# An attention and feed-forward kernel on one core: the accumulator bank of the second layer's h gets a tile of its own, and the seven output sums are paired anew in the other tiles

## The chip, the cores and the metric

The kernel runs on one core of a Trainium2 chip. The metric is the device time of one execution in microseconds. The engines that matter are PE (TensorE, with its weight loads PEld), ACT (ScalarE), DVE (VectorE) and SP, which issues all DMAs. PE writes its sums into PSUM, which has eight banks of 128 partitions x 512 floats; ACT and DVE read and write them there.

## The reference, cut to what matters

```
x = chunked softmax attention(q, k, v)          # 4608 tokens x 512
h = x @ moe_w_in;   g = elu(h);        x = g @ moe_w_out      # first layer, 512 -> 2048 -> 512
h = x @ moe2_w_in                                             # second layer
g = where(h >= 1, h, where(h <= -1, 0, (h + 1)**2 / 4))
out = g @ moe2_w_out
```

## The kernel before, in words

Tokens go in nine blocks of 512. The first layer runs plainly: 12 matmuls of 128x512 per slice of h (L682) and 12 per slice into four sums (L712), each factor split into a high and a low part.

The second layer uses a 2x2 scheme with seven products in place of eight. For each block b it takes eight steps (s counts them, 72 in all). A step works on two 128-wide slices of the hidden layer and two halves of the tokens. Its **products** (L774, in `step2`) are summed in one PSUM bank, called `hb`, whose two halves of 256 columns serve as two running sums. PE issues four runs of products per step:

- `first`, 12 matmuls. ACT then copies half 1 aside to z (`aside`, L797) and copies half 0 over half 1 (`seed(1)`, L800).
- `second`, 12 matmuls. ACT then reads half 0 into raw (`keep`, L806) and copies half 1 over half 0 (`seed(0)`, L800).
- `third`, 12 matmuls. DVE then adds z to both halves into raw (`right`, L809).
- `fourth`, 6 matmuls. ACT then reads half 1 into raw (`keep`, L806); after that `first` of the next step may write.

ACT and DVE apply the activation to raw and split it into a high and a low part (L819 to L838). The **output matmuls** (L935, in `outs`) take these as operands: 42 per step, six for each of the seven sums `T["out"][0..6]`, each sum in a PSUM bank of its own. They stand between the runs of products of the step that follows, in pieces of 13 (sums 0, 1 and the first matmul of sum 2, behind `second`), 9 (behind `third`), 7 (behind `fourth`) and 13 (behind `first`). A step so has 84 matmuls of 128x256 on PE. The seven sums grow over the eight steps of a block; at its end ACT copies sums 0 and 2 (L977) and DVE adds sums 3, 4, 1 (L985) and, last, 5 and 6 (L1022) for the stores (L991), while the next block's products run on. ACT and DVE also prepare the next block's input then (L639, L643, L629).

A planner (`Plan`) places all operations by costs and due times, and so sets the order on each engine; its operations on the engine "X" only hand out buffers. The order is then written out, and a recording layer gives each instruction the semaphore waits that its tiles call for. A tile is what `ps` or `pair` returns: `ps("h", i, ...)` is one bank, `pair("a", i, ...)` and `pair("acc", i, ...)` two banks under one name. There are eight banks: tile a0 (2), h0 and h1 (1 each), acc0 and acc1 (2 each). The first layer and the attention use them first, and `shared_banks` hands them on to the second layer.

Of the kernel before, what the change touches and what calls it, by code (L numbers as in the profile page):

```python
# [16 lines left out]
P = 128  # L17
BLK = 512
# [89 lines left out]
def chunk_attention_moe_moe2(ctx, tc, qk, v, w1, w2, w3, w4, out):  # L108
# [18 lines left out]
    NU = NT // P  # L127
# [22 lines left out]
    T = {}  # L150
# [9 lines left out]
    def ps(tag, i, shape, name):  # L160
        T[name] = pp.tile(shape, F32, tag=f"{tag}{i}", name=f"{tag}{i}")
        return T[name]

    def pair(tag, i, name):

        return ps(tag, i, [P, 2, BLK], name)
# [940 lines left out]
    def shared_banks():  # L1107
        last = L1 - 1
        T["out"] = [None] * 7

        def front(i):
            two = pair("a", i, "two")
            T["hb"], T["out"][0] = two[:, 0], two[:, 1]

        def middle(*i):
            for k in range(2):
                T["out"][1 + k] = ps("h", i[k], [P, BLK], "one")

        def back(k):
            def fn(i):  # L1120
                two = pair("acc", i, "two")
                T["out"][k], T["out"][k + 1] = two[:, 0], two[:, 1]
            return fn

        yield Op("X", 0.0, front, after=[("x", NU - 1)], take=("a",), event="hb")
        yield Op("X", 0.0, lambda: None, after=[], event=("free", 0, 0))
        yield Op("X", 0.0, middle, after=[("in", last)], take=("h",) * 2, event=("free", 0, 1))
        yield Op("X", 0.0, lambda: None, after=[], event=("free", 0, 2))
        yield Op("X", 0.0, back(3), after=[("half", last)], take=("acc",), event=("free", 0, 3))
        yield Op("X", 0.0, lambda: None, after=[], event=("free", 0, 4))  # L1130
        yield Op("X", 0.0, back(5), after=[("out", last)], take=("acc",), event=("free", 0, 5))
        yield Op("X", 0.0, lambda: None, after=[], event=("free", 0, 6))

# [24 lines left out]
    with tc.manual_schedule():  # L1160
# [4 lines left out]
        p = Plan(BUFS)  # L1165
        p.add(0, shared_buffers())
        p.add(L1, shared_banks())
        p.add(-40, first_loads())
        for u in range(NU):
# [80 lines left out]
```

## Time and profile before

| | |
|---|---|
| median of 3 runs | 1690.82 us |
| the profiled execution, its own time | 1690.58 us |
| its span, from the first to the last instruction | 1688.8 us |
| second layer alone on PE | about 896 to 1682 us of the span |
| PE busy / PE weight loads busy | 96% / 85% of the span |
| DVE / ACT busy | 61% / 58% |
| DMA, mean over the span | 160 GB/s |

The time of an execution lies 1.8 us above its span. A row of the timeline joins neighbouring instructions of one line; its first number is the start, and in brackets stands how long its engine had been idle and what ended that. The ends of matmuls are modelled: a matmul's modelled end lies past the start of the next one, so that differences of starts are the surer measure on PE.

### The profile page before, as it was taken

The numbers are of one execution on the slowest core, as the hardware profiler recorded it, in microseconds if no ns is written. First come the engines' busy times: TensorE is split into PE (matmuls) and PEld (weight loads), VectorE is DVE, ScalarE is ACT, GpSimd is POOL, SyncE is SP. The second block draws the span as 40 slices with busy tenths as digits, with TensorE's granted clock in tenths as the row PEclk, the third lists the DMA queues.
The fourth block names the chain that finished last, engine by engine and source line by source line (L and its number), as shares of the span: only waits on it lengthen the run. The fifth ranks groups of instructions, "written<-read, shape, count | busy, mean of one in ns | idle before, by whom it ended". The sixth has DMA issues, their size and how long they took to land.

```text
span 1688.8 us, 30552 instructions
## 1 busy us (share of the span) xinstructions
PE 1620.3 (96%) x11952; PEld 1430.1 (85%) x11952; DVE 1034.1 (61%) x1902; ACT 983.1 (58%) x2008; POOL 0.7 (0%) x6
## 2 busy tenths in 40 slices
PE   6999999999999999999999999999999999999998
PEld 5788888888888888888888999898989898989897
DVE  8992555555565555656335675757575757575665
ACT  6883444544555554555335666666666766666664
POOL 0000000000000000000000000000000000000000
PEclk9999999999999999999999999999999999999999
DMA  8640332433343434424656565656565656566565
GB/s 288 202 135 1 119 100 88 150 113 121 129 126 125 129 116 130 138 83 137 213 187 193 176 210 170 212 174 213 171 215 169 208 179 201 184 189 189 169 193 162
DMA packets 172497, 270.45 MB, mean 160 GB/s; under 512 B 15168, under 2 KB 78656, under 8 KB 172352
## 3 DMA queue, kind: packets, MB, share of 16 engines
q1 hardware_dynamic: 172352, 268.50, 50.3%
q8 instruction: 94, 1.54, 0.4%
q14 instruction: 51, 0.42, 0.1%
HBM read 219.15 MB, written 49.28 MB: 159 GB/s over the span
## 4 chain that ended last, share of the span: by engine, by line
PE 89%; ACT 6%; DVE 4%; issue 1%; DMA 0%; SPq 0%; DVEq 0%; ACTq 0%
PE acc L712 24%; PE h L682 24%; PE a L774 19%; PE acc L935 10%; PE h L935 5%; PE a L935 4%; ACT raw L806 2%; PE a L522 1%; ACT v L819 1%; ACT xu L639 1%; PE a L460 1%; DVE m L985 1%; PE h L502 1%; ACT m L977 0%; ACT high L835 0%
## 5 line engine op out<-in xcount | busy, mean ns | idle before, releaser
L774 PE MATMUL a<-xu,w 128*128 128x256 f32 x3024 | 409.4, 283 | 10.6 <-ACT raw L806 6.9
L774 PEld LDWEIGHTS a<-xu,w 128*128 128x128 f32 x3024 | 378.3, 188 | 17.2 <-ACT raw L806 8.5
L712 PE MATMUL acc<-gh,w 128*128 128x512 f32 x1152 | 297.4, 396 | 0.3 <-ACT gh L700 0.3
L682 PE MATMUL h<-xh,w 128*128 128x512 f32 x1152 | 292.3, 395 | 2.9 <-ACT w L249 1.6
L682 PEld LDWEIGHTS h<-xh,w 128*128 128x128 f32 x1152 | 216.3, 188 | 54.6 <-ACT w L249 1.8
L712 PEld LDWEIGHTS acc<-gh,w 128*128 128x128 f32 x1152 | 215.9, 188 | 51.5 <-ACT gh L700 0.8
L689 ACT ACTIVATE t<-h 128x512 f32<-128x512 f32 x144 | 86.0, 597 | 277.6 <-DVE gl L703 177.5
L935 PE MATMUL acc<-w,high 128*128 128x256 f32 x1728 | 240.1, 281 | 0.8 <-DVE m L985 0.8
L826 DVE SCALAR_TENSOR_TENSOR raw<-v,raw 128x256 f32<-128x256 f32 (+1 forms) x216 | 110.5, 512 | 202.4 <-ACT v L823 200.9
L935 PEld LDWEIGHTS acc<-w,high 128*128 128x128 f32 x1728 | 220.5, 188 | 1.0 <-DVE m L985 1.0
L703 DVE TENSOR_TENSOR gl<-t,gh 128x512 fp32r<-128x512 f32 x144 | 99.3, 689 | 174.7 <-PE acc L712 159.6
L838 DVE TENSOR_TENSOR high<-raw,high 128x512 fp32r<-128x512 f32 (+1 forms) x288 | 169.9, 620 | 24.3 <-ACT high L835 18.6
L697 DVE SCALAR_TENSOR_TENSOR t<-t,h 128x512 f32<-128x512 f32 x144 | 98.9, 687 | 136.8 <-ACT t L693 136.1
L835 ACT ACTIVATE high<-raw 128x512 fp32r<-128x512 f32 (+1 forms) x288 | 153.4, 571 | 35.0 <-DVE raw L826 23.9
L712 PE MATMUL acc<-gl,w 128*128 128x512 f32 x576 | 165.1, 400 | 0.0
L682 PE MATMUL h<-xl,w 128*128 128x512 f32 x576 | 157.3, 394 | 0.0
L819 ACT ACTIVATE v<-raw,half 128x256 f32<-128x256 f32 (+1 forms) x216 | 122.9, 573 | 46.3 <-DVE raw L809 46.3
L682 PEld LDWEIGHTS h<-xl,w 128*128 128x128 f32 x576 | 108.4, 188 | 25.7
L700 ACT ACTIVATE gh<-t 128x512 fp32r<-128x512 f32 x144 | 90.0, 625 | 64.6 <-PE acc L712 57.3
L712 PEld LDWEIGHTS acc<-gl,w 128*128 128x128 f32 x576 | 106.1, 188 | 24.5
L935 PE MATMUL h<-w,high 128*128 128x256 f32 x864 | 125.8, 281 | 0.1
L935 PEld LDWEIGHTS h<-w,high 128*128 128x128 f32 x864 | 112.7, 188 | 0.3 <-DVE high L838 0.3
(91 smaller groups left out, 1507.5 us busy)
## 6 DMA issues: line engine op xcount, KB each, us to landing
w<-w4s SPq DMA_DIRECT2D x504, 256.0 KB, 2.8
raw<-w SPq DMA_DIRECT2D x32, 512.0 KB, 7.3
qk<-qk SPq DMA_DIRECT2D x32, 512.0 KB, 4.8
m<-w SPq DMA_DIRECT2D x64, 256.0 KB, 3.4
w<-w3s SPq DMA_DIRECT2D x28, 512.0 KB, 4.0
w3s<-m SPq DMA_DIRECT2D x48, 256.0 KB, 2.5
w4s<-m SPq DMA_DIRECT2D x48, 256.0 KB, 2.7
v<-v SPq DMA_DIRECT2D x36, 256.0 KB, 3.2
```

Source lines behind the costliest of these rows:

```text
L682: nc.tensor.matmul(h, lhsT=w[:, wi, c, :], rhs=x[:, c, :], start=n == 0, stop=n == 3 * NC_ - 1)
L689: nc.scalar.activation(sb("t", i, [P, BLK], F32, ("act", s)), T["h", s], AF.Relu, scale=-1.0)
L697: nc.vector.scalar_tensor_tensor(out=t, in0=t, scalar=-1.0, in1=T["h", s], op0=ALU.add, op1=ALU.max)
L700: nc.scalar.activation(sb("gh", i, [P, BLK], F32R, ("gh", s)), T["act", s], AF.Copy)
L703: nc.vector.tensor_sub(sb("gl", gi, [P, BLK], F32R, ("gl", s)), T["act", s], T["gh", s])
L712: nc.tensor.matmul(T["acc", 0, b, m], lhsT=w[:, wi, m, :], rhs=T[g, s], start=first and (wi, g) == (0, "gh"), stop=last and g == "gl",)
L774: nc.tensor.matmul(half(q), lhsT=w[:, wi, c, :], rhs=x[:, c, :], start=start and k == 0, stop=clean and k == 5, skip_group_check=True,)
L819: nc.scalar.activation(t, part(), AF.Relu, bias=half_bias, scale=0.5)
L826: nc.vector.scalar_tensor_tensor(out=part(), in0=T["tt", s, ev], scalar=1.0, in1=part(), op0=ALU.min, op1=ALU.max)
L835: nc.scalar.activation(to(), of(), AF.Copy)
L838: nc.vector.tensor_sub(to(), of(), top())
L935: nc.tensor.matmul(T["out"][k][:, j * HB:(j + 1) * HB], lhsT=operand(k, s, lo)[:, j * P:(j + 1) * P], rhs=T["wo", 7 * s + k][:, wi], start ...
```

## The change

Only `shared_banks` is changed, which decides in which tile each of the second layer's eight banks lies.

| bank | tile before | tile after |
|---|---|---|
| `hb` | a0, with sum 0 | an h tile, alone |
| sum 0 | a0, with `hb` | a0, with sum 4 |
| sum 1 | an h tile, alone | acc, with sum 2 |
| sum 2 | an h tile, alone | acc, with sum 1 |
| sum 3 | acc, with sum 4 | acc, with sum 5 |
| sum 4 | acc, with sum 3 | a0, with sum 0 |
| sum 5 | acc, with sum 6 | acc, with sum 3 |
| sum 6 | acc, with sum 5 | an h tile, alone |

```diff
-        def front(i):
-            two = pair("a", i, "two")
-            T["hb"], T["out"][0] = two[:, 0], two[:, 1]
-
-        def middle(*i):
-            for k in range(2):
-                T["out"][1 + k] = ps("h", i[k], [P, BLK], "one")
-
-        def back(k):
+        def one(i):
+            return ps("h", i, [P, BLK], "one")
+
+        def h_bank(i):
+            T["hb"] = one(i)
+
+        def single(i):
+            T["out"][6] = one(i)
+
+        def two(tag, x, y):
             def fn(i):
-                two = pair("acc", i, "two")
-                T["out"][k], T["out"][k + 1] = two[:, 0], two[:, 1]
+                t = pair(tag, i, "two")
+                T["out"][x], T["out"][y] = t[:, 0], t[:, 1]
             return fn
 
-        yield Op("X", 0.0, front, after=[("x", NU - 1)], take=("a",), event="hb")
-        yield Op("X", 0.0, lambda: None, after=[], event=("free", 0, 0))
-        yield Op("X", 0.0, middle, after=[("in", last)], take=("h",) * 2, event=("free", 0, 1))
-        yield Op("X", 0.0, lambda: None, after=[], event=("free", 0, 2))
-        yield Op("X", 0.0, back(3), after=[("half", last)], take=("acc",), event=("free", 0, 3))
...
+        def free(*ks):
+            return [("free", 0, k) for k in ks]
+
+        yield Op("X", 0.0, h_bank, after=[("in", last)], take=("h",), event="hb")
+        yield Op("X", 0.0, two("a", 0, 4), after=[("x", NU - 1)], take=("a",), events=free(0, 4))
+        yield Op("X", 0.0, single, after=[], take=("h",), events=free(6))
+        yield Op("X", 0.0, two("acc", 1, 2), after=[("half", last)], take=("acc",), events=free(1, 2))
+        yield Op("X", 0.0, two("acc", 3, 5), after=[("out", last)], take=("acc",), events=free(3, 5))
```

No instruction is added or removed. Inside the second layer no instruction changes its place on PE, ACT, DVE or SP; only the waits differ. At the change of layers, where `hb` now comes from an h tile that the first layer gives up late, the first step's runs of products move one place back among the first layer's last matmuls.

On PE, inside a block, where `second` ends and the piece of 13 output matmuls begins. In the names, xu and w0, w1 are operands, high0 and high1 the split activations, and the waits in brackets name the engine or the DMA queue whose semaphore is waited for. Before:

```order
L774 MATMUL a0_7492<-xu1_7523,w0_8_7926 128x256 [waits Activation_49]
L774 MATMUL a0_7492<-xu1_7523,w0_8_7926 128x256 x5
L774 MATMUL a0_7492<-xu1_7523,w1_7_8072 128x256 x6
L935 MATMUL a0_7492<-w1_3_7930,high0_3_7481 128x256 [waits DMAHW3_49,Activation_49]
L935 MATMUL a0_7492<-w1_3_7930,high0_3_7481 128x256 x3
L935 MATMUL a0_7492<-w1_3_7930,high0_3_7481 128x256 [waits DVE_49]
L935 MATMUL h1_8289<-w1_3_7930,high0_0_7478 128x256 [waits DMAHW4_49]
```

And after, at the same place:

```order
L774 MATMUL h1_8210<-xu1_7522,w0_8_7925 128x256 [waits Activation_49]
L774 MATMUL h1_8210<-xu1_7522,w0_8_7925 128x256 x5
L774 MATMUL h1_8210<-xu1_7522,w1_7_8071 128x256 x6
L935 MATMUL a0_8211<-w1_3_7929,high0_3_7481 128x256 [waits DMAHW3_49]
L935 MATMUL a0_8211<-w1_3_7929,high0_3_7481 128x256 x3
L935 MATMUL a0_8211<-w1_3_7929,high0_3_7481 128x256 [waits DVE_49]
L935 MATMUL acc1_8400<-w1_3_7929,high0_0_7478 128x256 [waits DMAHW4_49,Activation_49]
```

The wait of sum 0's first matmul for ACT is gone; before, it was for the `keep` (L806) that reads `hb` behind `second`. The wait for ACT that sum 1 now shows is for the activation's high part (L835), which sum 0's wait had covered.

On ACT, at the same place. v0 is a scratch tile of the activation. Before:

```order
L835 ACTIVATE high1_2_8374<-raw2_7477 128x512 [waits DVE_49]
L806 ACTIVATE raw0_7475<-a0_7492 128x256 [waits PE_49]
L800 ACTIVATE a0_7492<-a0_7492 128x256 [waits PE_49,Activation_49]
L819 ACTIVATE v0_8555<-raw0_7475,half_70 128x256
L835 ACTIVATE high0_3_7481<-raw0_7475 128x256 [waits DVE_49]
```

And after:

```order
L835 ACTIVATE high1_2_8374<-raw2_7477 128x512 [waits DVE_49]
L806 ACTIVATE raw0_7475<-h1_8210 128x256 [waits PE_49]
L800 ACTIVATE h1_8210<-h1_8210 128x256 [waits Activation_49]
L819 ACTIVATE v0_8555<-raw0_7475,half_70 128x256
L835 ACTIVATE high0_3_7481<-raw0_7475 128x256 [waits DVE_49,PE_49]
```

`seed(0)` (L800) no longer waits for PE, that is, for sum 0's six matmuls; the wait for PE that the last row gains is for the matmuls that read the old high0_3, and stood in L800's before.

On PE, in the first step of a block, around `fourth`, where sum 3 is begun and DVE still reads the old sum 5 (L1022). Before:

```order
L935 MATMUL acc1_8400<-w1_1_7847,high0_1_7479 128x256 [waits DMAHW3_49]
L935 MATMUL acc1_8400<-w1_1_7847,high0_1_7479 128x256 x3
L774 MATMUL a0_7492<-xu2_8202,w1_4_7961 128x256 [waits DVE_49]
L774 MATMUL a0_7492<-xu2_8202,w1_4_7961 128x256 x5
L935 MATMUL acc1_8400<-w1_1_7847,high0_5_7483 128x256 x2
```

And after:

```order
L935 MATMUL acc0_8403<-w1_1_7846,high0_1_7479 128x256 [waits DMAHW3_49]
L935 MATMUL acc0_8403<-w1_1_7846,high0_1_7479 128x256 x3
L774 MATMUL h1_8210<-xu2_8201,w1_4_7960 128x256 [waits DVE_49]
L774 MATMUL h1_8210<-xu2_8201,w1_4_7960 128x256 x5
L935 MATMUL acc0_8403<-w1_1_7846,high0_5_7483 128x256 [waits DVE_49]
```

Sum 3's last two matmuls gain a wait for DVE, for the L1022 that reads sum 5 in the same tile; that L1022 in turn gains a wait for PE, for sum 3's first four matmuls.

## Rows read from the trace of the kernel before

**Rows 1.** The page: busy time of each engine, and the chain that ended last.
```profile
PE 1620.3 (96%) x11952; PEld 1430.1 (85%) x11952; DVE 1034.1 (61%) x1902; ACT 983.1 (58%) x2008; POOL 0.7 (0%) x6
...
PE 89%; ACT 6%; DVE 4%; issue 1%; DMA 0%; SPq 0%; DVEq 0%; ACTq 0%
```

**Rows 2.** Stretches: start:end, length, busy PE, PEld, DVE, ACT, POOL, clock, DMA, GB/s.
```profile
400.00:800.00 400.00, 400.00 (x2689) 324.04 (x2688) 233.60 (x435) 205.00 (x392) 0.00 (x0) 1.00 0.38 123
1000.00:1200.00 200.00, 188.66 (x1535) 183.53 (x1534) 127.38 (x236) 131.29 (x292) 0.00 (x0) 1.00 0.61 190
```

**Rows 3.** Waits of PE, whole span: total us, times, longest us.
```profile
PE a L935 <- ACT raw L806: 35.1, 71, 0.7
...
PE a L774 <- ACT raw L806: 6.9, 8, 0.9
...
PE a L774 <- DVE raw L809: 2.8, 8, 0.4
...
PE acc L935 <- DVE m L985: 0.8, 1, 0.8
```

**Rows 4.** Timeline of one step inside a block, 1007 to 1020 us.
```profile
1006.98 1.66 ACT L835 ACTIVATE high<-raw 128x512 fp32r<-128x512 f32 x3
...
1007.62 1.58 PE L774 MATMUL a<-xu,w 128*128 128x256 f32 x12
...
1009.24 0.38 ACT L806 ACTIVATE raw<-a 128x256 f32<-128x256 f32 x1 [0.60 <-PE a L774]
1009.68 0.78 PEld L935 LDWEIGHTS a<-w,high 128*128 128x128 f32 x6 [0.68 <-ACT raw L806]
1009.68 0.99 PE L935 MATMUL a<-w,high 128*128 128x256 f32 x6 [0.47 <-ACT raw L806]
...
1010.50 0.99 PE L935 MATMUL h<-w,high 128*128 128x256 f32 x7
1010.76 0.37 ACT L800 ACTIVATE a<-a 128x256 f32<-128x256 f32 x1 [1.14 <-PE a L935]
...
1011.33 1.59 PE L774 MATMUL a<-xu,w 128*128 128x256 f32 x12
...
1012.96 0.69 DVE L809 TENSOR_TENSOR raw<-a,z 128x512 f32<-128x512 f32 x1 [0.51 <-PE a L774]
...
1013.82 0.87 PE L774 MATMUL a<-xu,w 128*128 128x256 f32 x6
...
1015.37 1.59 PE L774 MATMUL a<-xu,w 128*128 128x256 f32 x12
...
1018.34 1.58 PE L774 MATMUL a<-xu,w 128*128 128x256 f32 x12
...
1020.40 0.99 PE L935 MATMUL a<-w,high 128*128 128x256 f32 x6 [0.47 <-ACT raw L806]
```

**Rows 5.** Timeline around the change from one block to the next, 1228 to 1257 us.
```profile
1228.72 0.99 PE L935 MATMUL a<-w,high 128*128 128x256 f32 x6 [0.47 <-ACT raw L806]
...
1235.68 1.68 PE L774 MATMUL a<-xu,w 128*128 128x256 f32 x12 [0.87 <-ACT raw L806]
...
1240.80 0.98 PE L935 MATMUL a<-w,high 128*128 128x256 f32 x6 [0.47 <-ACT raw L806]
...
1244.71 0.69 DVE L809 TENSOR_TENSOR raw<-a,z 128x512 f32<-128x512 f32 x1 [1.21 <-ACT m L977]
...
1245.46 0.97 PE L774 MATMUL a<-xu,w 128*128 128x256 f32 x6 [0.35 <-DVE raw L809]
...
1252.49 0.97 PE L935 MATMUL a<-w,high 128*128 128x256 f32 x6 [0.67 <-ACT raw L806]
...
1256.37 0.68 DVE L1022 TENSOR_TENSOR m<-acc,m 128x512 f32<-128x512 f32 x1
```

More of the change, by code (lines that the diff above doesn't have):

```diff
@@ L1109, in shared_banks @@
         T["out"] = [None] * 7
-        def front(i):
-            two = pair("a", i, "two")
-            T["hb"], T["out"][0] = two[:, 0], two[:, 1]
-        def middle(*i):
-            for k in range(2):
-                T["out"][1 + k] = ps("h", i[k], [P, BLK], "one")
-        def back(k):
+        def one(i):
[5 more added lines that the diff above has]
+        def two(tag, x, y):
             def fn(i):
-                two = pair("acc", i, "two")
-                T["out"][k], T["out"][k + 1] = two[:, 0], two[:, 1]
-            return fn
-        yield Op("X", 0.0, front, after=[("x", NU - 1)], take=("a",), event="hb")
-        yield Op("X", 0.0, lambda: None, after=[], event=("free", 0, 0))
-        yield Op("X", 0.0, middle, after=[("in", last)], take=("h",) * 2, event=("free", 0, 1))
-        yield Op("X", 0.0, lambda: None, after=[], event=("free", 0, 2))
-        yield Op("X", 0.0, back(3), after=[("half", last)], take=("acc",), event=("free", 0, 3))
-        yield Op("X", 0.0, lambda: None, after=[], event=("free", 0, 4))
-        yield Op("X", 0.0, back(5), after=[("out", last)], take=("acc",), event=("free", 0, 5))
-        yield Op("X", 0.0, lambda: None, after=[], event=("free", 0, 6))
+                t = pair(tag, i, "two")
+                T["out"][x], T["out"][y] = t[:, 0], t[:, 1]
+            return fn
+        def free(*ks):
[5 more added lines that the diff above has]
+        yield Op("X", 0.0, two("acc", 3, 5), after=[("out", last)], take=("acc",), events=free(3, 5))
     def block(b, f0=0, f1=NF):
```

## The prediction

> **What bounds the kernel now.** I read the page first. PE is busy for 96% of the span and makes 89% of the chain that ended last; DVE and ACT are busy for about 60% [rows 1]. So only time on PE counts, and the question is whether PE has idle time that this change reaches. The stretches answer where to look: in the first layer PE is busy for 400 of 400 us, in the second for 188.66 of 200 [rows 2]. The first layer offers nothing; the second, some 785 us long, has gaps. The waits name them: 71 times, nearly once for each of the 72 steps, an output matmul into tile a waited for ACT's L806, 35.1 us in all; the other waits of PE there are 6.9, 2.8 and 0.8 us [rows 3].
>
> The timeline of one step shows that wait [rows 4]. `second` starts at 1007.62. ACT's `keep` (L806) starts at 1009.24, when the last product is in the bank, and takes 0.38. Only then, at 1009.68, does sum 0's first matmul start, and its weight load with it. Yet `keep` reads `hb`, and sum 0 is another bank: they share a tile, no data. The same tie binds ACT: `seed(0)` (L800) begins only at 1010.76, after sum 0's six matmuls.
>
> What does it cost per step? From 1011.33 to 1018.34 PE issues 12, 9, 6, 7, 12 and 13 matmuls, 59 in 7.01 us without a wait: 0.1188 us each. A step has 84, so 9.98 us; but sum 0 comes at 1009.68 and again at 1020.40, 10.72 us later. 0.74 us per step are lost. They lie here: `second` should hand over after 12 x 0.1188 = 1.43 us and does so after 2.06, a loss of 0.63; the six matmuls of sum 0 then take 0.82 in place of 0.71, since the first weight load is no longer hidden, a loss of 0.11. (The view of waits shows 0.47 for the 0.63, as matmul ends are modelled late.)
>
> At that restart a rule of the Trainium skill can be weighed. The row shows the weight load and its matmul starting together at 1009.68, the load's unit having been idle for 0.68 [rows 4]: nothing was loaded ahead during the wait. The skill (page "TensorE: Matmul & The Clock Gate", section "Step-by-step: what each phase is for") has PE pull weight loads ahead of matmuls still in flight. If that held across a semaphore wait, the 0.11 would have another cause and might stay, which is 71 x 0.11 = 7.8 us less gain; the trace speaks against it here.
>
> **The change part by part.** First, `hb` leaves tile a. Sum 0 no longer waits for `keep`, `seed(0)` no longer waits for sum 0. In 71 steps 0.74 us go: **52.5 us**.
>
> Where does the stall go, what is late next? `third` needs `seed(0)`. Counted from the start of `second`: `keep` starts at 1.62 and ends at 2.00, L800 follows (0.37) and is done by about 2.4; 0.06 later, the lag between L806's end and sum 0, PE can know it: 2.46. PE itself arrives at `third` after 25 matmuls, at 2.97. So 0.5 us of cover remain. Before `keep`, ACT has three L835 that end at 1008.64, 0.60 ahead of it [rows 4]. `fourth` needs `right`: L809 starts 1.63 after `third` (1011.33 to 1012.96), takes 0.69, and with 0.06 the bank is free at 2.38; PE arrives after 21 matmuls, at 2.49. That order of 2.38 and 2.49 is the same as before, since from `third` to the next `second` nothing changes. The next step's `second` follows `first` after 25 matmuls, also as before (1015.37 to 1018.34).
>
> Second, the block changes. From sum 0 at 1228.72 to 1240.80 and 1252.49 two steps take 23.77 us, 2.33 more than 2 x 10.72 [rows 5]. Part of this is `first` at 1235.68, idle for 0.87 behind a `keep` that stands on ACT behind the preparation of the next block's input. With the 0.16 that the view leaves out (0.63 - 0.47) and the restart's 0.11 it is 1.14, and the change doesn't touch it. The other 1.2 us come from ties that go or loosen: L809 idles until L977 has copied sum 0 from the same tile, which holds `fourth` for 0.35 more; L800 and all that follows it on ACT come earlier; sum 0's wait at 1252.49 is 0.67 in place of 0.47. I take 1.19 for each of the 8 changes of block: **9.5 us**, bounds 0 and 2.33 x 8 = 18.6.
>
> Third, the new pairs. Sum 3 now lies with sum 5. In the first step of a block PE begins sum 3 (four matmuls) ahead of `fourth`, and DVE must then read the old sum 5 (L1022) before sum 3's last two. L1022 can start when those four are in the bank. By `keep`'s 1.62 against 1.43 that is 0.19 after they are issued, that is, after `fourth` has started; it takes 0.68 [rows 5], and with 0.06 PE may go on 0.93 after `fourth` started, in place of 6 x 0.1188 = 0.71. That is 0.22 and a restart of 0.11, or 0.33 at 8 places: **-2.6 us**, bounds 0 and -2.6, as DVE's next work waits on ACT anyway. The other pairs read their partner early: sum 4 waits for the copy of sum 0, sum 5 for the adding of sum 3, each with a run of products in between; I count nothing, and if that cover were gone it would cost one such 0.33 each.
>
> Fourth, the end. In the last step no products lie between the outputs; sum 4 there waits 0.8 us for DVE to read its old partner, sum 3 [rows 3]. Now sum 5 waits for that reader, one sum later, so that six matmuls (0.71) cover most of it. But DVE's adding, not PE, closes the kernel. Between 0 and 1, I take **0.5 us**.
>
> Fifth, the change of layers. The first runs of products move back one place among first-layer matmuls that never let PE idle [rows 2]. **0**, bounds 1 us either way.
>
> Sum: 52.5 + 9.5 - 2.6 + 0.5 = 59.9 us. The profiled execution took 1690.58 (span 1688.8 and 1.8 around it), 0.24 below the median, so no correction: **1630.7 us**. Best end: 52.5 + 18.6 + 1 = 72, 1618.5. Worst end: no gain at the block changes, -2.6 and -1: 48.9, 1641.7.
>
> **The rivals.** *The wait moves to `third`, in part.* If ACT reaches `keep` later than now, `seed(0)` ends later; past 0.50 us PE stands at `third`. ACT is 66% busy in this layer [rows 2], and with a step 0.74 shorter 70%; for it speaks that L835 ends only 0.60 ahead of `keep`, against it that L835's inputs hang on the `third` before, whose distance to `keep` doesn't change. If half of the 0.74 went that way: 1690.6 - 26 - 7 = about 1657. Chance 0.07.
>
> *The change frees nothing*, because the order between the engines is kept by bank and the wait has another reason. Against it: the wait for ACT stands on sum 0's first matmul before and not after, and `hb` and sum 0 were never in one bank. Time 1690.6. The Trainium skill (page "PSUM — Partial Sum Buffer", section "PSUM bank collisions raise a hardware error") asks that engines be kept apart by bank and quadrant; by that alone the kernel before would already let sum 0 run beside `keep`, and there would be nothing to win. The 71 waits of [rows 3] say that here it is the tile that counts. Chance 0.03.
>
> *Slower: `seed(0)` becomes the bound of the step.* With PE, ACT and DVE running closer together, `third` would stand behind L800 on ACT in every step. It decides from the point where L800 ends 0.50 + 0.74 = 1.24 us later after `second` than in the sum above; there the time is the old one. At 1.7 us it costs 0.46 x 71 = 33 us, 1724. Nothing in [rows 4] comes near: all that stands ahead of L800 is done 0.60 early. Chance 0.03.
>
> **How the numbers follow.** Forecast 0.87, the rivals 0.07, 0.03 and 0.03. A measurement of this kernel can tell about 2% from no change, here 1657. The forecast lies below with all its range, the first rival half: faster 0.91; within 2% 0.06; slower 0.03. The range is the forecast's own, 1618 to 1642; it leaves out the 0.13 of the rivals.
>
> **What would show it.** Right: sum 0 follows `second` with no idle time, L800 follows L806 at once, and a step inside a block takes 9.98 us; the waits of PE keep one of about 0.9 us per block at `first`, and a new one of about 0.1 to 0.3 for L1022 appears. Wrong: a wait for L800 at `third`, steps above 10.1 us, 0.35 at `fourth` still there at block changes, or a second new wait for L985 or L977 by the new pairs. A granted clock below 1.00 would upset all; at 400 of 400 us busy it was 1.00 [rows 2].

## The result and the profile after

| | before | after |
|---|---|---|
| median of its runs | 1690.82 us (3 runs) | 1631.14 us (3 runs) |
| ratio after to before, 95% interval | | 0.9646 (0.9624 to 0.9668) |
| the profiled execution / its span | 1690.58 / 1688.8 us | 1631.14 / 1629.2 us |

Slow executions are left out: one before (5036.68 us), one after (1946.26 us, at a mean granted clock of 0.754) and the profiled one of late_all below (5759.90 us, at 0.262), whose trace is therefore of a second run. The kernel became 59.7 us faster, to 1631.14 us; 1630.7 us was forecast.

The page after, its busy times and its chain, against [rows 1]:

```profile
PE 1600.5 (98%) x11952; PEld 1426.9 (88%) x11952; DVE 1032.0 (63%) x1902; ACT 984.9 (60%) x2008; POOL 0.7 (0%) x6
...
PE 94%; DVE 2%; ACT 2%; DMA 1%; issue 0%; SPq 0%; DVEq 0%
```

ACT falls from 6% to 2% of the chain with the same busy time: not its work shrank but what waited for it. The stretch inside the second layer, after (start:end, length, busy PE, PEld, DVE, ACT, POOL, clock, DMA, GB/s), against [rows 2]:

```profile
1000.00:1200.00 200.00, 198.31 (x1662) 197.46 (x1661) 135.69 (x252) 141.85 (x315) 0.00 (x0) 1.00 0.66 205
```

PE is busy for 198.31 of 200 us, where it was 188.66, and gets 1662 matmuls done in place of 1535. The waits of PE after, against [rows 3]:

```profile
PE acc L460 <- DMA qk<-qk: 7.0, 3, 4.1
PE h L774 <- ACT raw L806: 6.8, 8, 0.8
```

The 35.1 us of output matmuls behind L806, the 2.8 behind L809 and the 0.8 behind L985 are gone from the view; what stays in the second layer is one wait of `first` per block and, as before, a single one of 0.9 us in its second step. One step in the timeline after, against [rows 4]:

```profile
1000.40 1.58 PE L774 MATMUL h<-xu,w 128*128 128x256 f32 x12
...
1001.71 0.78 PEld L935 LDWEIGHTS a<-w,high 128*128 128x128 f32 x6
1001.83 0.87 PE L935 MATMUL a<-w,high 128*128 128x256 f32 x6
1002.03 0.38 ACT L806 ACTIVATE raw<-h 128x256 f32<-128x256 f32 x1 [0.60 <-PE h L774]
...
1002.44 0.37 ACT L800 ACTIVATE h<-h 128x256 f32<-128x256 f32 x1
...
1003.37 1.59 PE L774 MATMUL h<-xu,w 128*128 128x256 f32 x12
...
1005.00 0.69 DVE L809 TENSOR_TENSOR raw<-h,z 128x512 f32<-128x512 f32 x1 [0.87 <-PE h L774]
...
1005.86 0.87 PE L774 MATMUL h<-xu,w 128*128 128x256 f32 x6
...
1006.77 0.39 ACT L806 ACTIVATE raw<-h 128x256 f32<-128x256 f32 x1 [0.32 <-PE h L774]
...
1010.38 0.87 PE L774 MATMUL h<-xu,w 128*128 128x256 f32 x6
```

Sum 0 starts 1.43 us after `second`, ahead of `keep`, with its weights loaded 0.12 earlier; L800 follows L806 by 0.41; from `second` to `second` (1010.38; the view ends there and counts 6 of its 12 matmuls) it is 9.98 us, the forecast. Around a change of block after, against [rows 5]:

```profile
1208.22 0.87 PE L774 MATMUL h<-xu,w 128*128 128x256 f32 x6
1208.68 0.63 ACT L639 ACTIVATE xu<-xs 128x512 fp32r<-128x512 f32 x1 [1.75 <-DVE xs L629]
...
1209.83 0.61 ACT L639 ACTIVATE xu<-xs 128x512 fp32r<-128x512 f32 x1
...
1210.35 0.36 ACT L806 ACTIVATE raw<-h 128x256 f32<-128x256 f32 x1
...
1210.76 1.71 PE L774 MATMUL h<-xu,w 128*128 128x256 f32 x12 [0.85 <-ACT raw L806]
...
1226.79 1.59 PE L774 MATMUL h<-xu,w 128*128 128x256 f32 x12
...
1227.98 0.69 DVE L985 TENSOR_TENSOR m<-m,m 128x512 f32<-128x512 f32 x1
...
1228.59 0.69 DVE L809 TENSOR_TENSOR raw<-h,z 128x512 f32<-128x512 f32 x1
...
1229.33 0.97 PE L774 MATMUL h<-xu,w 128*128 128x256 f32 x6
1229.47 0.69 DVE L1022 TENSOR_TENSOR m<-acc,m 128x512 f32<-128x512 f32 x1 [0.20 <-PE acc L935]
...
1230.22 0.51 PE L935 MATMUL acc<-w,high 128*128 128x256 f32 x2
```

`keep` starts 2.13 us after `fourth` (0.91 inside a block), behind the preparation of the next block's input, and `first` waits. One step later `fourth` starts 2.54 us after `third` where 21 matmuls are 2.49: L809 stood behind an L985 and ended at 1229.28. Sum 3's last two then start 0.89 after `fourth` in place of 0.71, when L1022 has read sum 5; the view of waits has no row for this. (This is the second step of the new block; the sums of its first step stand in it. The prediction calls it the first.)

Counted from aside to aside (the starts of L797), the three steps at a change of block took 12.07, 11.50 and 10.91 us before and take 11.08, 9.97 and 10.30 after, at all eight changes but the last, which before took 12.07, 11.32 and 10.83; the 45 steps between take 10.72 before and 9.97 after (means 10.720 and 9.975). From the first layer's last matmul to the last output matmul, 787.1 us became 726.7, 60.5 less; the first layer ended 1.1 us later: the attention's L460, which the change doesn't touch, waited 2.1 us longer for DMA (and 1.5 us less for DVE).

### The profile page after: what moved, and what is told of

Same layout as the page of the kernel before. It is cut to its first block, busy times and chain, and to the rows that moved or that the text cites. A ratio compares the mean times of both kernels' runs of the same rounds, so it can differ in the third digit from the quotient of the medians.

```text
span 1629.2 us, 30555 instructions
## 1 busy us (share of the span) xinstructions
PE 1600.5 (98%) x11952; PEld 1426.9 (88%) x11952; DVE 1032.0 (63%) x1902; ACT 984.9 (60%) x2008; POOL 0.7 (0%) x6
## 4 chain that ended last, share of the span: by engine, by line
PE 94%; DVE 2%; ACT 2%; DMA 1%; issue 0%; SPq 0%; DVEq 0%
PE acc L712 25%; PE h L682 24%; PE h L774 21%; PE acc L935 11%; PE a L935 6%; PE h L935 3%; PE a L522 1%; PE a L460 1%; ACT xu L639 1%; PE h L502 1%; DMA qk<-qk 1%; ACT v L819 1%; DMA v<-v 0%; ACT raw L806 0%; DVE xu L643 0%
## 5 line engine op out<-in xcount | busy, mean ns | idle before, releaser
L774 PE MATMUL h<-xu,w 128*128 128x256 f32 x3024 | 408.1, 282 | 7.7 <-ACT raw L806 6.8
L774 PEld LDWEIGHTS h<-xu,w 128*128 128x128 f32 x3024 | 378.6, 188 | 11.0 <-ACT raw L806 8.4
L935 PE MATMUL acc<-w,high 128*128 128x256 f32 x1728 | 252.0, 282 | 0.3
L935 PEld LDWEIGHTS acc<-w,high 128*128 128x128 f32 x1728 | 225.3, 188 | 1.7 <-DVE high L838 0.3
L835 ACT ACTIVATE high<-raw 128x512 fp32r<-128x512 f32 (+1 forms) x288 | 153.2, 571 | 36.5 <-DVE raw L826 26.2
L935 PE MATMUL a<-w,high 128*128 128x256 f32 x864 | 137.4, 282 | 0.0
L935 PEld LDWEIGHTS a<-w,high 128*128 128x128 f32 x864 | 117.0, 188 | 0.0
```

Source lines behind the costliest of these rows:

```text
L774: nc.tensor.matmul(half(q), lhsT=w[:, wi, c, :], rhs=x[:, c, :], start=start and k == 0, stop=clean and k == 5, skip_group_check=True,)
L835: nc.scalar.activation(to(), of(), AF.Copy)
L935: nc.tensor.matmul(T["out"][k][:, j * HB:(j + 1) * HB], lhsT=operand(k, s, lo)[:, j * P:(j + 1) * P], rhs=T["wo", 7 * s + k][:, wi], start ...
```

## The experiments

The theory: the 0.74 us per step are a wait that the program makes because `hb` and sum 0 share a tile; what a tie costs is set by when the partner is written and read, so that any other partner has a price of its own, which the timeline tells. Rivals: only sum 0's place mattered; the new pairing has a part in the gain; `seed(0)` has no cover. Each kernel is the changed one with the edit that is named; the three called late_ start from pairs_56. In the edits `single(k)` puts sum k in a tile alone and `with_h(k)` puts `hb` and sum k in one tile; their definitions are left out. Where an edit shifts line numbers, the new ones are given.

**h_with_3.** `hb` shares its tile with sum 3.

```diff
-        yield Op("X", 0.0, h_bank, after=[("in", last)], take=("h",), event="hb")
-        yield Op("X", 0.0, two("a", 0, 4), after=[("x", NU - 1)], take=("a",), events=free(0, 4))
-        yield Op("X", 0.0, single, after=[], take=("h",), events=free(6))
+        yield Op("X", 0.0, with_h(3), after=[("x", NU - 1)], take=("a",), events=["hb"] + free(3))
+        yield Op("X", 0.0, single(0), after=[("in", last)], take=("h",), events=free(0))
+        yield Op("X", 0.0, single(4), after=[], take=("h",), events=free(4))
...
-        yield Op("X", 0.0, two("acc", 3, 5), after=[("out", last)], take=("acc",), events=free(3, 5))
+        yield Op("X", 0.0, two("acc", 5, 6), after=[("out", last)], take=("acc",), events=free(5, 6))
```

> hb shares its two-bank tile with sum 3 in place of sum 0; sums 0 and 4 are alone, the other pairs are 1+2 and 5+6. Theory (the tie is by tile, and costs what the partner's timing makes of it): sum 0 follows `second` at once, but sum 3's first four matmuls stand ahead of `fourth` and now wait for `right` (L809, ready 2.37 us after the start of `third`, PE there at 2.02), and its last two wait for the `keep` behind `fourth`: about 0.46 and 0.74 us per step, so steps of about 11.15 us in place of 9.97 and a time near 1713 us, slower than the kernel before. Rival (only that hb left sum 0 matters, or the waits go by bank): steps of 9.97 us and a time near 1630 us.

Measured: 1713.83 us, ratio 1.0137 (1.0120 to 1.0154); steps of 11.17 us. Its timeline:

```profile
1003.23 1.58 PE L774 MATMUL a<-xu,w 128*128 128x256 f32 x12
...
1004.85 0.69 DVE L809 TENSOR_TENSOR raw<-a,z 128x512 f32<-128x512 f32 x1 [0.86 <-PE a L774]
...
1005.59 0.73 PE L935 MATMUL a<-w,high 128*128 128x256 f32 x4 [0.20 <-DVE raw L809]
...
1006.16 0.88 PE L774 MATMUL a<-xu,w 128*128 128x256 f32 x6
1007.08 0.38 ACT L806 ACTIVATE raw<-a 128x256 f32<-128x256 f32 x1 [0.78 <-PE a L774]
...
1007.51 0.51 PE L935 MATMUL a<-w,high 128*128 128x256 f32 x2 [0.47 <-ACT raw L806]
```

Sum 3's four start 2.36 after `third` (the theory's 2.37), its last two 1.35 after `fourth` in place of 0.71. Two banks under one name cost 0.74 us per step as `hb` and sum 0, and 1.20 as `hb` and sum 3: slower than the kernel before. The rival falls.

**h_with_6.** `hb` with sum 6; sums 3 and 5 alone, pairs 1+2 and 0+4 (the same edit with other numbers).

> hb shares its tile with sum 6, whose six matmuls come last of the 13 behind `first`; sums 3 and 5 are alone, the other pairs are 1+2 and 0+4. Theory (tie by tile): the six are due 2.26 us after the start of `first`, `seed(1)` (L800) on the same tile is done at about 2.47, so 0.21 and a restart of 0.11, 0.32 us per step: steps of 10.29 us, 1650 to 1657 us. Rival (any place other than sum 0's is free): 9.97 us and 1630 us. Rival (sharing with any sum costs the old 0.74): 10.7 us and 1690 us.

Measured: 1656.38 us, one run; steps of 10.29 us. Two rows of its timeline, and its wait at the changes of block:

```profile
1003.39 0.37 ACT L800 ACTIVATE a<-a 128x256 f32<-128x256 f32 x1
...
1003.82 0.98 PE L935 MATMUL a<-w,high 128*128 128x256 f32 x6
```

```profile
PE a L774 <- DVE m L1022: 3.0, 8, 0.4
```

The price of 0.32 per step was met to 0.01; at the upper end of the range lies the time since `first` now also waits for L1022, which reads the old sum 6.

**h_with_0.** The new pairing alone: `hb` stays with sum 0; sums 4 and 6 alone, pairs 1+2 and 3+5.

> The new pairing without the own tile: hb stays with sum 0 as in the kernel before; sums 4 and 6 are alone, the other pairs are 1+2 and 3+5. Theory (the gain inside a block is all from hb's own tile): steps of 10.72 us and about 1690 us (1686 to 1694). Rival (the re-pairing has a part in it): steps below 10.5 us and a time under 1680 us.

Measured: 1695.22 us, one run; steps of 10.72 us, and 11.25 where the kernel before has 10.91. Its wait for `keep`:

```profile
PE a L935 <- ACT raw L806: 35.0, 71, 0.7
```

and its timeline where sum 3 is begun at a change of block:

```profile
1260.47 0.87 PE L774 MATMUL a<-xu,w 128*128 128x256 f32 x6
...
1261.41 0.30 PEld L935 LDWEIGHTS acc<-w,high 128*128 128x128 f32 x2 [0.28 <-DVE m L1022]
```

All of the old wait is there. The time is 1.2 us above the range: the second layer began 2.9 us later in this run than in the kernel before, 1.7 of it in longer waits of the attention's L460 for DMA. The eight steps that are 0.34 longer are the new wait for L1022, 2.7 us: `fourth` is on time here (1260.47, 2.51 after `third`), and sum 3's last two start 0.94 behind it. So the pairing brings nothing inside a block and loses where it was expected to.

**pairs_plain.** The own tile alone: `hb` and sum 0 each alone, the sums paired as they are counted.

```diff
-        yield Op("X", 0.0, two("a", 0, 4), after=[("x", NU - 1)], take=("a",), events=free(0, 4))
-        yield Op("X", 0.0, single, after=[], take=("h",), events=free(6))
-        yield Op("X", 0.0, two("acc", 1, 2), after=[("half", last)], take=("acc",), events=free(1, 2))
-        yield Op("X", 0.0, two("acc", 3, 5), after=[("out", last)], take=("acc",), events=free(3, 5))
+        yield Op("X", 0.0, two("a", 1, 2), after=[("x", NU - 1)], take=("a",), events=free(1, 2))
+        yield Op("X", 0.0, single(0), after=[], take=("h",), events=free(0))
+        yield Op("X", 0.0, two("acc", 3, 4), after=[("half", last)], take=("acc",), events=free(3, 4))
+        yield Op("X", 0.0, two("acc", 5, 6), after=[("out", last)], take=("acc",), events=free(5, 6))
```

> The own tile for hb without the new pairing: hb alone, sum 0 alone, pairs 1+2, 3+4, 5+6 as the sums are counted. Theory (the pairing costs only the 0.33 us at 8 places where sum 3 waits for the reading of sum 5, and that pair is gone here): steps of 9.97 us, none of 10.30, about 1629 us (1627.5 to 1630.5), 2.6 us less than the changed kernel less 0.5 us at the end where sum 4 waits for L985 again. Rival (the pairing by time pays): over 1633 us, with waits of PE for L985, L977 or L1022 that the changed kernel doesn't have.

Measured: 1630.16 us, ratio 0.9642 (0.9627 to 0.9656), the same as the changed kernel within the intervals. The pairing by time pays nothing. One detail missed: the step expected at 9.97 took 10.20, since `fourth` started 0.14 us late behind L809 and lost 0.09 more in its restart. The end showed, as expected, its 0.8 us for L985.

**pairs_56.** Sum 3 alone, 5 and 6 together, the rest as in the change.

```diff
-        yield Op("X", 0.0, single, after=[], take=("h",), events=free(6))
+        yield Op("X", 0.0, single(3), after=[], take=("h",), events=free(3))
...
-        yield Op("X", 0.0, two("acc", 3, 5), after=[("out", last)], take=("acc",), events=free(3, 5))
+        yield Op("X", 0.0, two("acc", 5, 6), after=[("out", last)], take=("acc",), events=free(5, 6))
```

> As the changed kernel, but sums 3 and 6 exchanged: sum 3 alone, sums 5 and 6 together (hb alone, 0+4, 1+2 unchanged). The new wait of sum 3 for the reading of sum 5 goes, by that also the 0.18 us that it costs at each change of block; the 0.15 to 0.23 us for which `fourth` stands there behind L809, as the plain pairing's run shows it, stays, since L809 stands on DVE behind two L985. Theory: steps of 9.97 us, 10.20 in place of 10.30 once per block, no wait for L985 at the end: 1629.5 us (1628.5 to 1631). As worked out ahead of these runs, with the whole 0.33 laid to L1022, it would be 1628.5 us with no step over 9.98 but the 11.09. Rival (the pairs matter by more than these waits): 2 us or more away from 1630.

Measured: 1629.35 us, ratio 0.9633 (0.9620 to 0.9646). The step of 10.30 became 10.13. Its timeline there:

```profile
1225.87 1.59 PE L774 MATMUL h<-xu,w 128*128 128x256 f32 x12
...
1227.07 0.69 DVE L985 TENSOR_TENSOR m<-m,m 128x512 f32<-128x512 f32 x1
...
1227.67 0.69 DVE L809 TENSOR_TENSOR raw<-h,z 128x512 f32<-128x512 f32 x1
...
1228.41 0.99 PE L774 MATMUL h<-xu,w 128*128 128x256 f32 x6
```

So of the 0.32 by which this step is longer in the changed kernel (10.30 against 9.975) 0.17 are the tie of sums 3 and 5, and 0.15 are L809 behind L985. In time the kernel is not to be told from the changed one; the steps tell it.

**late_56.** pairs_56, with the last three units of the next block's input behind the last `keep` of the block.

```diff
         T["t3", b] = T[B[1]]
+        if b:
+            yield Op("X", 0.0, lambda: None, after=[("c21", b * NP - 1)])
         yield Op("V", 0.6, diff("t3", B[3], B[1]))
```

> pairs_56, and the last three units of the next block's input (4, 6, 5: their L639 on ACT and L643 on DVE) put behind the last `keep` of the block before. Theory (the 1.1 us that remain at `first` once per block are `keep` standing on ACT behind this preparation): the wait of 6.8 us of PE for L806 goes to nearly none, the 11.08 us step falls to about 10.0 to 10.2, 8 us less in all: about 1621 us (1619.5 to 1623.5). Rival (keep waits for something else, or the units are then late for `third`, which would show as a wait for L639 or L643): 1629 us or more.

Measured: 1620.49 us, ratio 0.9585 (0.9572 to 0.9598), with late_right below the fastest in this study. PE's wait for `keep` is gone from the view. Its timeline (`keep` is L808 here, products L776):

```profile
1203.87 0.87 PE L776 MATMUL h<-xu,w 128*128 128x256 f32 x6
...
1204.78 0.39 ACT L808 ACTIVATE raw<-h 128x256 f32<-128x256 f32 x1
...
1205.42 1.59 PE L776 MATMUL h<-xu,w 128*128 128x256 f32 x12
...
1205.85 0.63 ACT L639 ACTIVATE xu<-xs 128x512 fp32r<-128x512 f32 x1 [0.17 <-DVE xs L629]
```

`keep` starts 0.91 after `fourth`, as inside a block, and L639 follows. The two steps of 11.08 and 9.97 became 10.24 and 9.70, together 2 x 9.97: nothing is lost there now, 1.11 x 8 = 8.9 us.

**seed2 and seed4.** `seed(0)` issued two and four times; the same copy, so that the same is computed.

```diff
-        yield Op("A", 0.31, lambda: seed(0), event=("seeded2", s))
+        def seeds():
+            for _ in range(2):
+                seed(0)
+
+        yield Op("A", 0.31, seeds, event=("seeded2", s))
```

> The changed kernel with `seed(0)` issued twice in every step (the same copy again, 0.28 to 0.42 us more on ACT ahead of `third`). Theory (0.5 us of cover): hidden, steps of 9.97 us, 1630 to 1633 us. Rival (there is no cover, ACT's chain from keep to seed(0) is level with PE): steps of 10.25 to 10.4 us, 1651 us or more.

> The same with `seed(0)` issued four times (0.84 to 1.26 us more). Theory (0.5 us of cover, then every 0.01 us counts, and a restart of 0.11): `third` waits 0.34 to 0.76 and 0.11 in each step, steps of 10.4 to 10.85 us, 1663 to 1693 us. Rival (much more cover than 0.5): 9.97 us and 1631 us.

Measured, one run each: 1636.04 us with steps of 9.98, and 1693.58 us with steps of 10.79. In seed2 the copy is hidden in the steps; the time is 3 us over the range, since the steps at a change of block grew (11.37 and 10.42 in place of 11.08 and 10.30, 3.3 us together) and the first layer ended 1.4 us later. The timeline of seed4:

```profile
1043.19 1.59 PE L774 MATMUL h<-xu,w 128*128 128x256 f32 x12
...
1045.23 1.57 ACT L800 ACTIVATE h<-h 128x256 f32<-128x256 f32 x4
...
1046.85 1.49 PEld L774 LDWEIGHTS h<-xu,w 128*128 128x128 f32 x12 [0.74 <-ACT h L800]
1046.85 1.71 PE L774 MATMUL h<-xu,w 128*128 128x256 f32 x12 [0.54 <-ACT h L800]
```

Three more copies take 1.57 - 0.37 = 1.20 us on ACT; the step grew by 0.82, of which 0.11 is the restart. 1.20 - 0.71 = 0.49: the cover of 0.5 us was sized right.

**late_all, late_all_again, late_right.** late_56, with the two L985 that need no sum put behind an L809, so that `fourth` no longer stands behind it.

```diff
+        if s + 1 < NP * NB:
+            yield Op("X", 0.0, lambda: None, after=[("right", s + 1)])
         yield Op("V", 0.6, more2)
```

> late_56, and at a change of block the two L985 that need no sum (and so L1022 and their stores behind them) put behind L809 of the next block's first step. Theory (the 0.15 us that `fourth` still loses there is L809 standing on DVE behind these L985): the step of 10.13 us falls to 9.97 to 10.0, 1.2 us less than late_56's 1620.5: 1619.3 us (1618 to 1621), seen in the steps rather than in the time. Rival (L809 was late for another reason, or L1022, now 1.4 us later, holds sum 5 up in its turn): the step stays at 10.1 or more, 1620.5 us or more.

Measured: 1636.57 us, ratio 0.9678 (0.9664 to 0.9691), 16 us over late_56: a miss. The edit named the L809 of the wrong step. The trace is of a second run:

> late_all once more for a trace at full clock. Its 1636.5 us are 16 us over late_56, 2.0 us at each of 8 changes of block. Theory: the second step of a block is about 2.1 us longer, since the L809 that releases `fourth` stands behind two L1022 and one or two more operations of 0.4 to 0.7 us on DVE. Rival: the time lies at another step, or on a wait for `first`.

Measured: 1636.70 us; the second step of a block 12.26 us. Its waits (L840 is the activation's low part, L811 is `right`):

```profile
PE acc L937 <- DVE high L840: 12.2, 8, 1.5
...
PE h L776 <- DVE raw L811: 1.5, 7, 0.2
```

The place was right, the cause mostly not: with L985 and L1022 in new places on DVE, an operand of the output matmuls comes 1.5 us late, and L809 only 0.2. late_right names the second step's L809, `("right", s + 2)`:

> late_56 again with the two late L985 (and the L1022 behind them) put behind L809, now of the step in which `fourth` is held, the second of the new block; the edit of late_all named the first step's L809, and its order on DVE has both L1022 ahead of the L809 in question, four operations earlier than before. Theory: L809 no longer stands behind an L985, `fourth` starts on time, the step of 10.13 us falls to 9.97 to 10.0: 1.2 us less than late_56, 1619.3 us (1618 to 1621). Rival (L1022, now about 1.4 us later, holds up the new sum 5, or L809 was late for another reason): a step of 10.1 us or more, 1620.5 us or more.

Measured: 1620.65 us, ratio 0.9587 (0.9574 to 0.9600). Its timeline (L1026 is L1022 of the kernel before):

```profile
1222.22 0.69 DVE L811 TENSOR_TENSOR raw<-h,z 128x512 f32<-128x512 f32 x1
...
1223.08 0.87 PE L776 MATMUL h<-xu,w 128*128 128x256 f32 x6
...
1224.36 0.68 DVE L1026 TENSOR_TENSOR m<-acc,m 128x512 f32<-128x512 f32 x1
...
1225.56 0.68 DVE L1026 TENSOR_TENSOR m<-acc,m 128x512 f32<-128x512 f32 x1
```

```profile
1226.30 1.68 PE L937 MATMUL acc<-w,high 128*128 128x256 f32 x12
```

The second step takes 9.97 us, `fourth` is on time; but the next takes 10.21: the new sum 5 starts only at 1226.30, behind the second L1026. By the kernel's order that one reads the old sum 6, which lies in the same tile; the reader of the old sum 5, the first L1026, was done at 1225.04. The rival held, since the later addition does hold sum 5 up: the wait only moved, to the tie of sums 5 and 6. The same order with 5 and 6 in tiles of their own was not run.

## Why the prediction was right

**The 71 steps.** Forecast 71 x 0.74 = 52.5 us; the steps went from 10.720 to 9.975 (9.98 was said), 71 x 0.745 = 52.9. Cause shown: with `hb` bound to sum 0 the wait is back in full (h_with_0), with sum 6 or 3 it has the price that the timeline gives (0.32 and 1.20), with none the steps are 9.97, however the sums are paired (pairs_plain, pairs_56).

**The restart of 0.11.** Before, the weight load started only with its matmul after the wait; after, it starts 0.12 ahead (1001.71 and 1001.83). The rule that the Trainium skill gives (page "TensorE: Matmul & The Clock Gate", section "Step-by-step: what each phase is for"), that weight loads are pulled ahead of matmuls in flight, fits the stream without waits; across a wait no row shown here does: at 1046.85 of seed4 the weight load again starts only with its matmul. The 0.11 went with the wait, as forecast.

**What is late next.** The 0.5 us of cover for `seed(0)` held (seed2, seed4); neither `third` nor `fourth` waits inside a block.

**The changes of block.** The net was right: the eight changes cost 18.3 us beyond plain steps before (34.48 - 3 x 10.72 = 2.32 each, 2.06 the last) and 11.4 after (1.43 each), 6.9 less, where 9.5 - 2.6 = 6.9 was forecast. The wait of `first` stays at 1.11 (1.14 was said), and late_56 shows what it is. All else that was too long before went, 2.32 - 1.11 = 1.21 (1.19 was said): the step of 11.50, in which L977 had held L809 and so `fourth`, takes 9.97. The new 0.32 agrees with the 0.33 that was put down for sum 3's wait for L1022, but in part by luck. That price holds where `fourth` is on time: h_with_0, with the same pair, shows 0.34. In the changed kernel L809 stands on DVE behind an L985 in this step, which the prediction didn't name; it makes `fourth` late and costs 0.15, and so leaves only 0.17 to the tie (pairs_56).

**The end.** Forecast 0.5; the wait of 0.95 us behind L985 (0.8 in the view, [rows 3]) became one of 0.28, 0.67 less. From a timeline of the changed kernel's end:

```profile
1620.94 0.69 DVE L985 TENSOR_TENSOR m<-acc,m 128x512 f32<-128x512 f32 x1
...
1621.73 0.95 PE L935 MATMUL acc<-w,high 128*128 128x256 f32 x6
```

**The change of layers.** Forecast 0 within 1; the sum of the other terms, 52.9 + 6.9 + 0.7, is 60.5, as measured for the second layer, so nothing of size lies there. The first layer's end, 1.1 us later, was in no term.

**The rivals.** No wait of `third` stands in the view after. That order by bank would leave nothing to win fell with 71 waits gone. The Trainium skill (page "PSUM — Partial Sum Buffer", section "PSUM bank collisions raise a hardware error") asks for order within a bank and quadrant. The kernel before kept order between the two banks of a tile too, and that surplus, between `hb` and sum 0, is what the change removed. Whether less than a bank's order would do was not tried.

## What to carry to other kernels

Where waits are kept by tile, two banks under one name are one resource: put a bank that is read and seeded in every step alone, and price every other pairing by when the partner is written and read; a wrong partner (sum 3) cost more than the change gained per step. After removing a wait, look which operation on the releasing engine stands ahead of the next one that is waited for: ordering the block's input preparation behind the last `keep` gave 8.9 us more, and moving DVE's additions gave nothing, since the wait moved on to the tie of sums 5 and 6; moved behind the wrong step's L809 they cost 16 us.

## What the runs showed that was not expected

Two small waits in a row don't add as two terms: the later one shrinks by what the earlier one already cost (sum 3's wait for L1022 costs 0.34 with `fourth` on time and 0.17 behind a `fourth` that has already cost 0.15). And the attention's DMA waits at the start differ from run to run by more than a microsecond: between kernels with the same order there the first L797 came at 879.73 us (before) and 882.60 (h_with_0), or at 881.95 (after) and 880.43 (late_right, L799 there). L460's waits for DMA were 7.8 and 9.5 us, or 9.9 and 8.1. This limits what single runs can tell.
